# Attention and a gated MLP on one core: a list scheduler for all engines, half-blocks of 64 keys in eight array tiles, norms on VectorE and DMA

## The chip, the cores and the metric

One NeuronCore of a Trainium2 chip runs the whole kernel. Its engines work at the same time and are kept together by semaphores: TensorE (PE in the profile; its weight loads are PEld) multiplies from SBUF into PSUM, VectorE (DVE) and ScalarE (ACT) read PSUM, GpSimd (POOL) works on SBUF alone, and SyncE (SP) only issues DMAs. PSUM has eight banks of 128 partitions by 512 float32 values. TensorE's array can be used as a whole or as tiles of 32 or 64 rows or columns, each with weights of its own. The metric is the device time of one execution in microseconds (us), the median of several.

## The reference

With x of 2048 tokens by 512, the kernel computes x + A(xn) + B(xn), where xn is x normalised over its 512 features:

```
def _A_ref(x, wqkv, wo):
    H = 32; Dh = D // H; W = 256
    q, k, v = qkv[0], qkv[1], qkv[2]
    scores = jnp.einsum("bhqd,bhkd->bhqk", q, k) * (Dh ** -0.5)
    mask = (idx[:, None] - idx[None, :] >= 0) & (idx[:, None] - idx[None, :] < W)
    p = softmax(where(mask, scores, -1e9))
    return einsum("bhqk,bhkd->bhqd", p, v) ... @ wo
def _B_ref(x, w_gate, w_up, w_down):
    return ((x @ w_gate) * (x @ w_up)) @ w_down
```

There are 32 heads of 16 features, a causal window of 256 keys, and a hidden width of 1792. Inputs and output are bf16.

## The kernel before

Tokens go in four chunks of 512, and a chunk's work has two strands. The attention strand handles a chunk T, a group c of eight heads and a parity par of the heads (24 steps to a chunk). A score step (`scores`, L201) multiplies blocks of 128 keys with the queries that see them, for four heads at once: head e sits on 32 partitions, so four row tiles of the array (`tile_position=(32*e, 0)`) work side by side, each into a PSUM bank of its own. `Ko` is K with the even heads set to zero, which picks the odd head of a 32-row tile. The three steps of a parity (`GROUPS`) cover the twelve visible blocks in strips of 512 columns. ACT takes the exponential of the strip into P (L209), POOL sets the masked triangles to zero (L214, L218), and two steps later `values` (L234) multiplies P with V on four column tiles into the bank `accb`; a seventeenth column of ones gives the softmax's sum. DVE transposes the result in squares of 32 (L245), divides (L247, L248) and after both parities transposes back into `OT` (L251).

The dense strand is a list of "fillers" with costs in matmuls (`fillers`): projections (`proj_v`, `proj_qk`), 14 gate and up pairs (`gate`, `up`; DVE copies the gate to `gsb`, then multiplies the up sum by it into `hT`), the down sums with the output projection added in the same bank (`down`, `finish`), the result added to x and stored (`store`). The next chunk's norms hang between gates: `norm_stats`, `norm_scale`, `norm_apply`, and `norm_transpose`, which transposes xn on TensorE and copies it to `xnT`. Dense work shares three PSUM banks (`ps_m`), S has four, `accb` one.

The order is that of the program: `run` emits the first chunk's norms and projections block by block, then for each step the scores, the values of two steps before, and as many fillers as keep their share of the whole. Every engine executes its instructions in the order in which they were emitted. Loads of x and the MLP weights go through SP's queue, Wqkv in three parts through ACT's. Down sums of the last chunk run without the last head group; `finish_late` adds that part from a bank of its own.

## Time and profile before

| | |
|---|---|
| time, median of 3 runs | 301.23 us (301.23 to 304.61) |
| span of the profiled execution | 299.1 us, from the first to the last instruction |
| what lies around the span (median less span) | 2.1 us |
| busy: TensorE, DVE, ACT, POOL | 92%, 65%, 61%, 52% of the span |
| granted TensorE clock, mean | 0.996 |

The span is what the trace shows; the time of a run also has the start and end of the execution around it. Busy times of matmuls are their recorded durations, and since matmuls are pipelined, the price of one is read from start to start. The rest of the document uses "dense" for matmuls on the whole array.

### The profile page before, as it was taken

The page shows a single profiled execution, that of the slowest core. Times are in us where ns is not written, and L with a number is a line of the kernel's source. Part 1 is how long each engine was busy: PE and PEld are TensorE (multiplying, and loading weights), DVE is VectorE, ACT ScalarE, POOL GpSimd, SP SyncE. Part 2 cuts the span into 40 slices and gives each one's busy share as a digit, 9 for nine tenths or more (in the row PEclk, how much of TensorE's full clock was granted, in tenths as well). Part 3 has the DMA queues.
Part 4 walks back from the last instruction along what each step waited for, and adds up shares of the span by engine and source line. Part 5 has one row for each costly group of instructions (what it writes and reads, how often), then busy time and mean ns, then how long its engine had stood idle before and what let it go on. Part 6 is the DMA issues. An engine that isn't in the chain of part 4 may idle for free.

```text
span 299.1 us, 5877 instructions
## 1 busy us (share of the span) xinstructions
PE 274.7 (92%) x2424; PEld 119.6 (40%) x2460; DVE 194.3 (65%) x362; ACT 181.5 (61%) x118; POOL 156.8 (52%) x266
## 2 busy tenths in 40 slices
PE   6569989999999999999999999999999999999992
PEld 5333333433433444444344444443444443344440
DVE  3238898985823599984942489985763357877325
ACT  1247566568766756669566666758766675756610
POOL 3115565455565556656555466655556555555620
PEclk9999999999999999999999999999999999999998
DMA  7999000000000100000000000000000000000001
GB/s 234 370 369 324 3 3 0 3 0 2 1 20 18 37 0 2 1 2 2 0 19 19 20 18 3 0 2 1 2 0 20 35 20 1 2 0 2 2 0 70
DMA packets 10506, 12.17 MB, mean 41 GB/s; under 512 B 496, under 2 KB 10480, under 8 KB 10480
## 3 DMA queue, kind: packets, MB, share of 16 engines
q1 hardware_dynamic: 8896, 10.23, 10.1%
q10 hardware_dynamic: 1584, 1.57, 1.7%
q8 instruction: 19, 0.31, 0.4%
q14 instruction: 7, 0.06, 0.1%
HBM read 9.70 MB, written 2.10 MB: 39 GB/s over the span
## 4 chain that ended last, share of the span: by engine, by line
PE 68%; ACT 17%; DVE 6%; DMA 3%; issue 3%; POOL 1%; ACTq 1%; DVEq 0%
ACT P L209 16%; PE psd L279 15%; PE up L270 12%; PE gp L261 11%; PE S L201 10%; PE accb L234 7%; PE qkp L167 6%; DMA Wqkv<-in_A_wqkv_dram 3%; PE vp L157 2%; PE psd L284 2%; DVE at L245 1%; PE xTp L145 1%; DVE hT L272 1%; DVE st L114 1%; PE qkb L183 1%
## 5 line engine op out<-in xcount | busy, mean ns | idle before, releaser
L209 ACT ACTIVATE P<-S 128x2048 bf16<-128x2048 f32 (+2 forms) x96 | 170.0, 1771 | 86.8 <-PE S L201 79.1
L214 POOL TENSOR_SCALAR_AFFINE_SELECT P<-P 128x512 bf16<-128x512 bf16 x128 | 81.8, 639 | 75.2 <-ACT P L209 74.6
L218 POOL TENSOR_SCALAR_AFFINE_SELECT P<-P 128x512 bf16<-128x512 bf16 x112 | 72.8, 650 | 42.4 <-ACT P L209 42.4
L261 PE MATMUL gp<-xnT,Wg 128*128 128x512 bf16 x213 | 57.1, 380 | 1.4 <-DVE gsb L264 0.5
L270 PE MATMUL up<-xnT,Wu 128*128 128x512 bf16 x216 | 57.3, 380 | 0.5
L279 PE MATMUL psd<-Wd,hT 128*128 128x512 bf16 x213 | 51.7, 380 | 1.4 <-issue 1.3
L272 DVE TENSOR_TENSOR hT<-up,gsb 128x512 bf16<-128x512 f32 x56 | 38.5, 687 | 11.0 <-PE up L270 8.0
L245 DVE STREAM_TRANSPOSE at<-accb 128x512 f32<-128x512 f32 x32 | 22.9, 715 | 32.6 <-PE accb L234 32.2
L264 DVE CAST gsb<-gp 128x512 bf16<-128x512 f32 x56 | 38.1, 680 | 3.7 <-PE gp L261 3.4
L270 PEld LDWEIGHTS <-Wu 128*128 128x128 bf16 x224 | 19.9, 98 | 25.8 <-issue 5.4
L279 PEld LDWEIGHTS <-hT 128*128 128x128 bf16 x224 | 19.8, 97 | 25.9 <-issue 5.3
L261 PEld LDWEIGHTS <-Wg 128*128 128x128 bf16 x224 | 19.8, 98 | 25.0 <-issue 6.0
L167 PE MATMUL qkp<-xnT,Wqkv 128*128 128x512 bf16 x117 | 27.5, 380 | 0.5 <-issue 0.5
L234 PE MATMUL accb<-P,V 128*17 128x384 bf16 (+2 forms) x704 | 25.4, 276 | 0.0
L291 DVE TENSOR_TENSOR y<-psd,x 128x512 bf16<-128x512 f32 x12 | 8.3, 692 | 23.2 <-PE psd L284 23.2
L201 PE MATMUL S<-Q,Ko 32*128 32x256 bf16 (+2 forms) x352 | 18.4, 275 | 3.8 <-ACT P L209 3.6
L201 PE MATMUL S<-Q,K 16*128 16x256 bf16 (+2 forms) x352 | 18.4, 275 | 2.6 <-ACT P L209 2.4
L234 PEld LDWEIGHTS <-V 128*17 128x17 bf16 x704 | 13.8, 90 | 8.7 <-issue 5.5
L167 PEld LDWEIGHTS <-Wqkv 128*128 128x128 bf16 x120 | 10.7, 98 | 13.7 <-issue 2.5
L157 PE MATMUL vp<-Wqkv,xnT 128*128 128x512 bf16 x61 | 15.9, 392 | 0.3 <-issue 0.2
L201 PEld LDWEIGHTS <-Ko 32*128 32x128 bf16 x352 | 6.9, 92 | 22.6 <-issue 22.1
L201 PEld LDWEIGHTS <-K 16*128 16x128 bf16 x352 | 6.6, 92 | 22.6 <-issue 22.5
(44 smaller groups left out, 172.2 us busy)
## 6 DMA issues: line engine op xcount, KB each, us to landing
out_dram<-y SPq DMA_DIRECT2D x16, 128.0 KB, 1.7
Wg<-in_B_w_gate_dram SPq DMA_DIRECT2D x2, 896.0 KB, 9.9
Wu<-in_B_w_up_dram SPq DMA_DIRECT2D x2, 896.0 KB, 11.5
Wd<-in_B_w_down_dram SPq DMA_DIRECT2D x1, 1792.0 KB, 17.7
Wqkv<-in_A_wqkv_dram ACTq DMA_DIRECT2D x3, 512.0 KB, 6.0
x<-in_A_x_dram SPq DMA_DIRECT2D x1, 1024.0 KB, 14.6
x<-in_A_x_dram SPq DMA_DIRECT2D x4, 128.0 KB, 5.1
x<-in_A_x_dram SPq DMA_DIRECT2D x1, 512.0 KB, 8.2
```

Source lines behind the costliest of these rows:

```text
L167: nc.tensor.matmul(ps[:], lhsT=self.Wqkv[:, k, lo:lo + 128], rhs=self.xnT[T][:, k, :], start=(k == 0), stop=(k == 3))
L201: nc.tensor.matmul(S[:, e, col:col + n], lhsT=(self.Ko if par else self.K)[U][rows, c, 128 * j:128 * j + 128], rhs=self.Q[T][rows, c, 128 ...
L209: nc.scalar.activation(out=P[:, :, lo:hi], in_=S[:, :, lo:hi], func=ACT.Exp, scale=0.25)
L214: nc.gpsimd.affine_select(out=P[:, :, j:j + 128], in_=P[:, :, j:j + 128], pattern=[[0, 4], [1, 128]], compare_op=ALU.is_ge, fill=0.0, base ...
L218: nc.gpsimd.affine_select(out=P[:, :, j:j + 128], in_=P[:, :, j:j + 128], pattern=[[0, 4], [-1, 128]], compare_op=ALU.is_gt, fill=0.0, bas ...
L234: nc.tensor.matmul(acc[32 * e:32 * e + 17, 128 * q0:128 * q0 + n], lhsT=self.V[U][:, v, 8 * c + 2 * e + par, 0:17], rhs=P[:, e, col:col + ...
L245: nc.vector.transpose(out=at.rearrange("p b r -> p (b r)"), in_=acc[:])
L261: nc.tensor.matmul(ps[:], lhsT=self.Wg[:, k, 128 * f:128 * f + 128], rhs=self.xnT[T][:, k, :], start=(k == 0), stop=(k == 3))
L264: nc.vector.tensor_copy(out=self.gsb[:], in_=ps[:])
L270: nc.tensor.matmul(ps[:], lhsT=self.Wu[:, k, 128 * f:128 * f + 128], rhs=self.xnT[T][:, k, :], start=(k == 0), stop=(k == 3))
L272: nc.vector.tensor_tensor(out=self.hT[T][:, f, :], in0=ps[:], in1=self.gsb[:], op=ALU.mult)
L279: nc.tensor.matmul(self.psd[:], lhsT=self.hT[T][:, f, 128 * b:128 * b + 128], rhs=self.Wd[:, f, :], start=(f == 0), stop=False)
```

## The change

The whole program is written anew, around a scheduler in the file. `Op`, `Dense` and `Sums` are pieces of work with their inputs, engines and costs; `loop` places them one after another by estimated times (`choose` picks what TensorE does next: values, scores, or dense work from two lists A and B), and emits each when it is placed. So the order on every engine comes from the file's costs. Copies from PSUM may go to DVE or ACT, whichever the estimates favour. Four things change in the work itself.

Blocks of keys are 64 wide. `layout` deals the half-blocks to two lanes, even and odd, and a batch holds 512 columns of each lane: five batches for a pair (T, c) in chunks 1 to 3, four in chunk 0. Scores use eight tiles of 32 rows by 64 columns, values eight of 64 rows by 32 columns. In phase 0 of a pair's values lane 0 does the even heads and lane 1 the odd ones, each into its own bank, in phase 1 the other way round; TensorE is drained between the phases and a semaphore, `turn`, holds phase 1 back. A pair's two transposes, the reciprocal, the product and the transpose back follow together on DVE. POOL's selects work on one lane's 64 partitions and may span several half-blocks.

PSUM has S (four banks) and four banks M for everything else; a value pair takes two of them. The first chunk goes by blocks, with the third part of Wqkv moved to SP's queue. Later norms no longer pass through TensorE: DVE applies them, and `dma_start_transpose` on SP's queue writes `xnT`. In the last chunk the four down sums wait in four banks and Wo is added to them in place.

```diff
+    order = {
+        (0, 0): ((0, 2), (2, 4, 6)), (0, 1): ((1, 3), (3, 5, 7)),
+        (1, 0): ((-4, -2, 4), (0, 2), (2, 6)), (1, 1): ((-3, -1, 3), (1, 3), (5, 7)),
+    }
...
+    if T == 0:
+        plan = [((par, n, 0),) for par in range(2) for n in range(2)]
+    else:
+        plan = [((0, 0, 0),), ((0, 1, 0),), ((0, 2, 0), (1, 2, 4)), ((1, 0, 0),), ((1, 1, 0),)]
...
+        self.M = [psum.tile([128, 512], F32, name=f"M{i}") for i in range(4)]
...
-        for t in range(4):
-            nc.sync.dma_start(out=self.x[:, t, :], in_=xv[:, t, :])
-        for lo in (1024, 512, 0):
-            nc.scalar.dma_start(out=self.Wqkv[:, :, lo:lo + 512], in_=wq[:, :, lo:lo + 512])
-        nc.sync.dma_start(out=self.x[:, 4:8, :], in_=xv[:, 4:8, :])
+        load(nc.sync, self.x[:, 0, :], xv[:, 0, :])
+        load(nc.scalar, self.Wqkv[:, :, 1024:1536], w["qkv"][:, :, 1024:1536])
+        load(nc.sync, self.x[:, 1, :], xv[:, 1, :])
+        load(nc.scalar, self.Wqkv[:, :, 512:1024], w["qkv"][:, :, 512:1024])
+        load(nc.sync, self.x[:, 2, :], xv[:, 2, :])
+        load(nc.sync, self.x[:, 3, :], xv[:, 3, :])
+        load(nc.sync, self.Wqkv[:, :, 0:512], w["qkv"][:, :, 0:512])
...
-                nc.tensor.matmul(S[:, e, col:col + n],
-                                 lhsT=(self.Ko if par else self.K)[U][rows, c, 128 * j:128 * j + 128],
-                                 rhs=self.Q[T][rows, c, 128 * q0:128 * q0 + n],
-                                 start=True, stop=True, tile_position=(32 * e, 0),
-                                 skip_group_check=True)
+        for at, lane, par, k, q, m in sorted(todo):
+            U, j = divmod(8 * T + k, 8)
+            for e in range(4):
+                rows = slice(32 * e, 32 * e + (32 if par else 16))
+                self.nc.tensor.matmul(
+                    self.S[64 * lane:64 * lane + 64, e, 64 * at:64 * (at + m)],
+                    lhsT=(self.Ko if par else self.K)[U % 3][rows, c, 64 * j:64 * j + 64],
+                    rhs=self.Q[T % 2][rows, c, 64 * q:64 * (q + m)],
+                    start=True, stop=True, tile_position=(32 * e, 64 * lane), skip_group_check=True)
...
-                    nc.gpsimd.affine_select(out=P[:, :, j:j + 128], in_=P[:, :, j:j + 128],
-                                            pattern=[[0, 4], [1, 128]], compare_op=ALU.is_ge,
-                                            fill=0.0, base=0, channel_multiplier=-1)
+    def i_select(self, P, lane, kind, at, n, step):
+        v = P[64 * lane:64 * lane + 64].rearrange("p e (b q) -> p e b q", q=64)
+        v = v[:, :, at:at + (n - 1) * step + 1:step, :]
+        sign = -1 if kind else 1
+        self.nc.gpsimd.affine_select(out=v, in_=v, pattern=[[0, 4], [0, n], [sign, 64]], base=0, fill=0.0,
+                                     compare_op=ALU.is_gt if kind else ALU.is_ge, channel_multiplier=-sign)
...
-                    nc.tensor.matmul(acc[32 * e:32 * e + 17, 128 * q0:128 * q0 + n],
-                                     lhsT=self.V[U][:, v, 8 * c + 2 * e + par, 0:17],
-                                     rhs=P[:, e, col:col + n], start=first, stop=(i == 2),
-                                     tile_position=(0, 32 * e), skip_group_check=True)
+        if phase == 1:
+            self.nc.tensor.wait_ge(self.turn, self.v)
+        todo = []
+        for lane in range(2):
+            par, at0 = lane ^ phase, 0
+            for P, batch in strips:
+                for p, k, q, m, at in batch[lane]:
+                    if p == par:
+                        todo.append((at0, lane, par, k, q, m, at, P))
+                        at0 += m
+        for _, lane, par, k, q, m, at, P in sorted(todo, key=lambda t: t[:2]):
+            U, j = divmod(8 * T + k, 8)
+            for e in range(4):
+                self.nc.tensor.matmul(
+                    banks[par][32 * e:32 * e + 17, 64 * q:64 * (q + m)],
+                    lhsT=self.V[U % 3][64 * lane:64 * lane + 64, j // 2, 8 * c + 2 * e + par, 0:17],
+                    rhs=P[64 * lane:64 * lane + 64, e, 64 * at:64 * (at + m)],
+                    start=(par, e) not in begun, stop=phase == 1, tile_position=(64 * lane, 32 * e),
+                    skip_group_check=True)
+                begun.add((par, e))
+        if phase == 0:
+            self.nc.tensor.drain().then_inc(self.turn, 1)
...
-        for g, s in enumerate(steps):
-            fill(-1, g)
-            self.scores(*s)
-            values(g - LAG)
-            done_w += weight[g]
-            fill(total * done_w / sum(weight), g)
+    def loop(self):
+        while True:
...
+                    at = max(t, self.free[e])
+                    key = (at + (0.3 if e == "A" and len(o.on) > 1 else 0.0), o.rank, t)
+                    if best is None or key < best[0]:
+                        best = (key, o, e, at)
+            p = self.choose()
+            if p is not None and (best is None or p[0] <= best[3]):
+                self.do(*p)
...
+                break
+            _, o, e, at = best
+            took, lat = o.on[e]
+            o.start, o.eng, o.end = at, e, at + lat + LAT
+            self.free[e] = at + took
+            self.waiting.remove(o)
+            self.log.append((at, e, took, o.name))
+            if self.live:
...
+        hi = 64 * max(s[4] + s[3] for lane in batch for s in lane)
+        took = 0.000833 * 4 * hi
+        ex = self.op(f"exp{g}", {"A": (took + 0.06, took + 0.18)}, [o], lambda e: self.nc.scalar.activation(
+            out=P[:, :, 0:hi], in_=self.S[:, :, 0:hi], func=ACT.Exp, scale=0.25), rank=0)
...
+        for par in range(2):
+            t = self.op(f"tr{v}", {"V": (0.64, 0.74)}, [o] + ts, lambda e, par=par: nc.vector.transpose(
+                out=self.at[:, :, par, :], in_=self.M[banks[par]].rearrange("p (b r) -> p b r", r=32)), rank=1)
+            self.frees(t, banks[par])
+            ts = [t]
...
-        for k in range(4):
-            nc.tensor.transpose(ps[:, k, :], xn[:, 128 * k:128 * k + 128], self.ident[:])
...
+        st = [self.op(f"st{T}.{b}", {"V": (0.81, 0.9)}, begin, lambda e, b=b: self.i_stats(4 * T + b, self.mv[w]),
+                      rank=8) for b in range(4)]
...
+            ap = self.op(f"ap{T}.{b}", {"V": (0.32, 0.41)}, [r], lambda e, b=b: self.i_apply(4 * T + b), rank=7)
+            deps = [ap] + ([("up", T - 2, NF - 1)] if T > 1 else [])
+            self.at_["xnT", T, b] = self.op(f"dt{T}.{b}", {"S": (1.5, 3.0)}, deps, lambda e, b=b: (
+                self.nc.sync.dma_start_transpose(out=self.xnT[w][:, :, 128 * b:128 * b + 128], in_=self.xn[b][:])),
+                rank=1)
...
-        for b in range(4):
-            self.finish_late(NCH - 1, b)
+        late = [] if b < 2 else [("attended", T)]
+        self.B.insert(len(self.B) - b, Sums(name, T, b, 0, NF, h + late, 7, emit, lambda o, i: None, link))
+        self.B.append(Sums("wo" + name, T, b, NF, 18, o, 4, emit, evac, link))
```

DVE at the start, from the first statistics on (`st`; `mv` holds mean and variance, `xn` the normalised block, `qkb` the first K and Q sums). Before:

```order
L114 BN_STATS st_169<-x_87 128x6
L115 BN_AGGR mv_168<-st_169 128x2
L114 BN_STATS st_177<-x_87 128x6
L115 BN_AGGR mv_176<-st_177 128x2
L133 TENSOR_SCALAR xn_184<-x_87,mv_168,rs_174 128x512
L185 CAST K0_164<-qkb_193 128x128
L186 CAST Q0_163<-qkb_193 128x128
L114 BN_STATS st_211<-x_87 128x6
L115 BN_AGGR mv_210<-st_211 128x2
L133 TENSOR_SCALAR xn_218<-x_87,mv_176,rs_182 128x512
```

The third block's statistics stand behind the first block's K and Q. DVE at the same place after the change:

```order
L267 BN_STATS st_189<-x_64 128x6
L268 BN_AGGR mv0_98<-st_189 128x2
L267 BN_STATS st_192<-x_64 128x6
L268 BN_AGGR mv0_98<-st_192 128x2
L267 BN_STATS st_197<-x_64 128x6
L268 BN_AGGR mv0_98<-st_197 128x2
L278 TENSOR_SCALAR xn0_94<-x_64,mv0_98,rs0_100 128x512
L267 BN_STATS st_203<-x_64 128x6
L268 BN_AGGR mv0_98<-st_203 128x2
L278 TENSOR_SCALAR xn1_95<-x_64,mv0_98,rs0_100 128x512
L278 TENSOR_SCALAR xn2_96<-x_64,mv0_98,rs0_100 128x512
L278 TENSOR_SCALAR xn3_97<-x_64,mv0_98,rs0_100 128x512
```

All four statistics and applies now come ahead of the first copy of K; the third block's statistics stand ahead of the first apply. SP's queue from the last loads on, before:

```order
L69 DMA x_87<-in_A_x_dram 128x8x512
L70 DMA Wd_92<-in_B_w_down_dram 128x14x512
L71 DMA Wo_89<-in_A_wo_dram 128x4x512
L292 DMA out_0_dram<-y_1140 128x512
L292 DMA out_0_dram<-y_1220 128x512
```

The stores follow the loads directly. SP at the same place after the change:

```order
L168 DMA Wo_66<-in_A_wo_dram 128x4x512
L632 DMA_TRANSPOSE xnT1_82<-xn0_94 128x4x128
L632 DMA_TRANSPOSE xnT1_82<-xn1_95 128x4x128
L632 DMA_TRANSPOSE xnT1_82<-xn2_96 128x4x128
L632 DMA_TRANSPOSE xnT1_82<-xn3_97 128x4x128
L632 DMA_TRANSPOSE xnT0_81<-xn0_94 128x4x128
L632 DMA_TRANSPOSE xnT0_81<-xn1_95 128x4x128
L632 DMA_TRANSPOSE xnT0_81<-xn2_96 128x4x128
L713 DMA out_0_dram<-y_1632 128x512
L632 DMA_TRANSPOSE xnT0_81<-xn3_97 128x4x128
L713 DMA out_0_dram<-y_1843 128x512
```

Two chunks' transposes stand ahead of the first stores, and one store stands within the second four.

## Rows read from the trace of the kernel before

**Rows 1.** The page: busy us, and the chain that ended last, by engine.
```profile
PE 274.7 (92%) x2424; PEld 119.6 (40%) x2460; DVE 194.3 (65%) x362; ACT 181.5 (61%) x118; POOL 156.8 (52%) x266
...
PE 68%; ACT 17%; DVE 6%; DMA 3%; issue 3%; POOL 1%; ACTq 1%; DVEq 0%
```

**Rows 2.** Windows: stretch, its us, busy us of each engine, clock, DMA.
```profile
21.40:294.30 272.90, 261.72 (x2326) 111.01 (x2360) 185.14 (x335) 175.99 (x109) 152.26 (x249) 1.00 0.05 17
0.00:21.40 21.40, 12.90 (x98) 8.61 (x101) 7.58 (x25) 5.56 (x9) 4.51 (x17) 1.00 0.97 323
```

**Rows 3.** The chain in order of time: start, us, what.
```profile
283.95 3.02 PE psd L279 x14
```

**Rows 4.** Timeline of PE, 100 to 105.9 us: start, us, instructions, idle before.
```profile
100.15 0.40 PE L201 MATMUL S<-Q,K 16*128 16x384 bf16 x8
...
102.61 0.40 PE L201 MATMUL S<-Q,Ko 32*128 32x128 bf16 x8 [0.23 <-ACT P L209]
102.94 1.04 PE L270 MATMUL up<-xnT,Wu 128*128 128x512 bf16 x4
...
104.68 1.03 PE L270 MATMUL up<-xnT,Wu 128*128 128x512 bf16 x4
105.64 0.40 PE L201 MATMUL S<-Q,Ko 32*128 32x256 bf16 x8
```

**Rows 5.** Timeline of PE, 105.5 to 108.5 us.
```profile
105.96 0.83 PE L234 MATMUL accb<-P,V 128*17 128x128 bf16 x24
106.73 1.04 PE L261 MATMUL gp<-xnT,Wg 128*128 128x512 bf16 x3
```

**Rows 6.** Waits of PE: us in total, times, longest us.
```profile
PE S L201 <- ACT P L209: 6.1, 23, 0.6
```

**Rows 7.** The four matmuls that begin the value step: durations (ns), and the timeline.
```profile
L234 PE MATMUL accb<-P,V x4: 224/224/226, 106.0 to 106.0; 128*17 128x128 bf16 x4
...
105.96 0.23 PE L234 MATMUL accb<-P,V 128*17 128x128 bf16 x4
```

**Rows 8.** DMA issues: count, KB each, median us to landing.
```profile
out_dram<-y SPq DMA_DIRECT2D x16, 128.0 KB, 1.7
...
x<-in_A_x_dram SPq DMA_DIRECT2D x4, 128.0 KB, 5.1
```

**Rows 9.** Timeline of DVE, 5 to 21.6 us, and PE's first score step.
```profile
5.58 0.69 DVE L114 BATCH_NORM_STATS2 st<-x 128x6 f32<-128x512 bf16 x1 [1.36 <-DMA x<-in_A_x_dram]
...
11.01 0.29 DVE L185 CAST K<-qkb 128x128 bf16<-128x128 f32 x1 [4.23 <-PE qkb L183]
...
11.42 0.68 DVE L114 BATCH_NORM_STATS2 st<-x 128x6 f32<-128x512 bf16 x1
...
12.23 0.38 DVE L133 TENSOR_SCALAR xn<-x,mv,rs 128x512 bf16<-128x512 bf16 x1
14.61 0.29 DVE L185 CAST K<-qkb 128x128 bf16<-128x128 f32 x1 [1.99 <-PE qkb L183]
...
21.40 0.34 PE L201 MATMUL S<-Q,K 16*128 16x384 bf16 x4
```

**Rows 10.** Groups by line and shape: busy us, mean ns of one, idle before.
```profile
L209 ACT ACTIVATE P<-S 128x2048 bf16<-128x2048 f32 x80 | 150.2, 1878 | 76.8 <-PE S L201 69.1 <-POOL P L218 6.4 <-POOL P L214 1.3
L214 POOL TENSOR_SCALAR_AFFINE_SELECT P<-P 128x512 bf16<-128x512 bf16 x128 | 81.8, 639 | 75.2 <-ACT P L209 74.6
...
L264 DVE CAST gsb<-gp 128x512 bf16<-128x512 f32 x56 | 38.1, 680 | 3.7 <-PE gp L261 3.4
...
L245 DVE STREAM_TRANSPOSE at<-accb 128x512 f32<-128x512 f32 x32 | 22.9, 715 | 32.6 <-PE accb L234 32.2
...
L78 POOL TENSOR_SCALAR_AFFINE_SELECT ident<-ident 128x128 bf16<-128x128 bf16 x1 | 0.3, 292 | 0.1
```

**Rows 11.** Timeline of DVE at the end: the last four results.
```profile
293.31 1.87 DVE L291 TENSOR_TENSOR y<-last,y 128x512 bf16<-128x512 f32 x3
295.83 0.69 DVE L291 TENSOR_TENSOR y<-last,y 128x512 bf16<-128x512 f32 x1 [0.66 <-DMA out_dram<-y]
```

More of the change, by code (lines that the diff above doesn't have):

```diff
@@ new lines, in selects @@
+def selects(batch):
+    out = []
+    for lane in range(2):
+        cols = {0: [], 4: []}
+        for _, k, q, m, at in batch[lane]:
+            for i in range(m):
+                if q + i - k in cols:
+                    cols[q + i - k].append(at + i)
+        for d, cs in cols.items():
+            cs.sort()
+            while cs:
+                run, step = 1, (cs[1] - cs[0] if len(cs) > 1 else 1)
+                while run < len(cs) and cs[run] - cs[run - 1] == step:
+                    run += 1
+                if run * step != 8:
+                    run = step = 1
+                out.append((lane, d // 4, cs[0], run, step))
+                cs = cs[run:]
+    return out
@@ new lines, in copy, with matmuls, i_scores @@
+    def copy(self, eng, out, in_):
+        if eng == "A":
+            self.nc.scalar.activation(out=out, in_=in_, func=ACT.Copy)
+        else:
+            self.nc.vector.tensor_copy(out=out, in_=in_)
+    def matmuls(self, ps, pairs, first=True, last=True):
+        for n, (a, b) in enumerate(pairs):
+            self.nc.tensor.matmul(ps, lhsT=a, rhs=b, start=first and n == 0, stop=last and n == len(pairs) - 1)
+    def i_scores(self, T, c, batch):
+        todo = [(at, lane, par, k, q, m) for lane in range(2) for par, k, q, m, at in batch[lane]]
+        for at, lane, par, k, q, m in sorted(todo):
+            U, j = divmod(8 * T + k, 8)
@@ new lines, in pe, with take_bank, frees, f @@
+    def pe(self, at, took, name, reader="V"):
+        o = Op(name, {}, [], None)
+        o.start, o.end = at, at + took + PE_LAT[reader]
+        self.now = at + took
+        self.log.append((at, "P", took, name))
+        return o
+    def take_bank(self):
+        i = min((t, i) for i, t in enumerate(self.banks) if t is not None)[1]
+        self.banks[i] = None
+        return i
+    def frees(self, op, i):
+        def f(o):
+            self.banks[i] = o.end
+        op.then.append(f)
+    def score_deps(self, g):
+        T, c, batch = self.batches[g]
+        deps = {("S", g - 1), ("Pfree", g - self.PBUFS)}
+        for lane in range(2):
+            for par, k, q, m, at in batch[lane]:
+                U, j = divmod(8 * T + k, 8)
+                deps |= {("Ko" if par else "K", U, c, j // 2), ("Q", T, c, q // 2), ("Q", T, c, (q + m - 1) // 2)}
+        return [d for d in deps if not (d[0] in ("S", "Pfree") and d[1] < 0)]
```

760 lines of the change are left out of this document (450 added, 310 removed), and 3 rows, old and new, of the table GROUPS.

## Prediction

> **What bounds the kernel now.** I read the page's busy shares and its chain first. TensorE is busy 92% of the span and holds 68% of the chain that ended last; no other engine passes 65% [rows 1]. Then the stretches: from the first score matmul (21.40 us) to the last matmul TensorE's records cover 261.7 of 272.9 us, at a granted clock of 1.00, 2.4 GHz [rows 2]. So in the body each microsecond is a slot of TensorE's, and the question is how many slots the change removes. The other places are the start, where TensorE is busy 12.9 of 21.4 us [rows 2], and the end, 4.9 us without matmuls.
>
> The timeline gives the price of a slot. Fourteen dense matmuls of 512 columns take 3.02 us, 0.216 each [rows 3]; 128 columns are then 0.054. A score step of 512 columns on each of four row tiles holds TensorE from 102.61 to 102.94, 0.33: its columns and 0.11 more. Four dense matmuls (0.86) ahead of a score step take 104.68 to 105.64, so going over costs 0.10 [rows 4]. A value step (1536 columns on each of four column tiles) takes 105.96 to 106.73, 0.77: 0.65 and 0.12 [rows 5]. I take 0.11 for each change between dense, score and value work.
>
> The ledger of the body before: 904 dense matmuls after the first score step (920 less the 16 of the first chunk's V), 195.0 us; 48 transposes of 128 columns, 2.6; scores, 80 steps of 512 columns, 8 of 384 and 8 of 256, 46,080 columns, 19.4; values, 24 steps of 1536 and 8 of 1152, again 46,080, 19.4; 225 changes, counted in the instruction order, 24.8. The sum is 261.2; the stretch is 272.9, so 11.7 us are waits. The largest is scores that wait for the exponential still reading S: 6.1 us in 23 waits [rows 6].
>
> **The change part by part.**
>
> *Half-blocks.* With blocks of 64 keys the band has less waste: a pair (a chunk and a group of eight heads) needs 20 half-blocks of 64 columns for each lane and parity where it had 12 blocks of 128. Two lanes side by side make 76 score batches of 512 columns for 96 steps: 38,912 columns, 16.4 us, 3.0 less. The values need 2560 columns a pair in chunks 1 to 3 and 2048 in chunk 0: 38,912 again, 3.0 less. This holds if eight tiles run at once. The trace has four at once, by rows and by columns, never both; I take full overlap, since each split by itself shows no cost beyond its columns and the change of mode [rows 4, 5]. The other end, no overlap, is a rival.
>
> *Small matmuls.* There are 3328 tiled matmuls for 1408. The four that begin a value step last 0.224 each and together 0.23 [rows 7]: their starts lie some 3 ns apart, so the 22 of a batch need about 0.07 of its 0.216 us, and the number costs nothing. The Trainium skill ("TensorE: Matmul & The Clock Gate", section "Wait — 56ns, not 53.3ns?") says that start-to-start never drops below about 25 ns, however small a matmul is. By that rule 3328 of them need 83 us, an estimate from the page, and the sum would end 50 us higher; the trace disagrees for matmuls on different tiles, with its 3 ns.
>
> *Changes of mode.* The new order has 198 for 225: 3.0 less. Sixteen drains of TensorE are new, one between the phases of each value pair. No drain is in the trace. Below, it costs nothing beyond the change that follows anyway; above I put 0.5, an estimate of two emptyings by the 0.22 to 0.23 that one small matmul lasts [rows 7]. It is nearest to a change of mode, so I take 0.15 each, 2.4.
>
> *Later norms by DMA.* 48 transposes leave TensorE, 2.6 us; nine of their copies leave DVE. Twelve DMA transposes of 128 KB are new, on SP. The nearest rows are the output stores of that size, 1.7 us to landing, and the x loads, 5.1 [rows 8]. Behind the last of chunk 1's applies the new order has nineteen gate and up groups ahead of the first projection that reads xnT1, 16.4 us, with seven score batches and two value pairs besides, some 21 us. Four transposes one after another take 6.8 by the stores and 20.4 by the loads, so they are hidden; above I allow 3 us, once (the later chunks have about 40 us). Stores queue behind them on SP and y has three buffers, but the transposes are issued before the next chunk's sums are due.
>
> *The start.* Before, DVE has the third block's statistics (11.42) behind block 0's copy of K, which waits 4.23 us; the blocks then go one after another, and the first scores start at 21.40 [rows 9]. The new order has all statistics early. But the third stands ahead of the first apply, and its x lands late: the second's statistics start at 5.58 [rows 9], and the median landing is 5.1 after an issue at some 2 to 3 us [rows 8], so I put the third at 7.9. Statistics to apply take 0.81, apply to the copy of K 2.38 [rows 9], and block 0's V now stands between, 0.86: 12.0. From there DVE has eleven copies up to block 2's Q, six of 128 columns at 0.29 [rows 9] and five of 512 at up to 0.68 [rows 10], 5.1 us: 17.1. I take 17.5 for the first scores; the ends are 16.1 (the third block lands a little sooner) and 21.4 (nothing gained).
>
> *The waits.* By slots, scores in the new order start at least 2.55 us apart; two that ACT alone holds apart start 2.46 apart (100.15 and 102.61, [rows 4]). So the 6.1 us should go; the other 5.6 stay. New is that a value pair holds two of four accumulators, where dense work had three to itself; I add 3, so 8.6.
>
> *Other engines.* ACT: 76 exponentials for 96, 142.7 us at 1.88 [rows 10], and 14 copies, less than before. DVE: ten gate casts and nine xnT copies go, fifteen V copies come, reciprocals and products are merged, some 9 us off its 194. POOL: 357 selects on 64 partitions for 240, 301 of them of 256 elements and 56 of 512; a select of 128 elements took 0.29, one of 512 0.64 [rows 10], so 0.41 and 0.64: 159 us, as now, off the path except as a rival.
>
> *The end.* Now the fourth y waits for a buffer and starts 3.3 us before the span ends [rows 11]. In the new order 49 dense matmuls, 10.6 us, and the sixteen of Wo follow the last values, so OT is ready in time and the y's follow sums 0.86 apart: 3.5 us behind the last matmul if no y waits for a buffer, 4.9 as now; I take 4.0.
>
> **The sum.** Dense 195.0, block 3's K and Q after the first scores 0.4, scores and values 32.8, 198 changes 21.8: 250.0. With 17.5 ahead, 2.4 of drains, 8.6 of waits and 4.0 behind it, the span is 282.5, for 299.1. The profiled execution's span lies 2.1 us under the median of 301.23, so the prediction is **284.6 us**, 5.5% less. Its own range: start -1.4 to +3.9, drains -2.4 to +5.6, waits -5 to +8, transposes up to +3; not all on one side, so 276 to 293.
>
> **The rivals.**
>
> *The lanes run one after the other* (slower). Scores use two column halves of one row group at once, values two row halves of one column group. If such a pair shares a path, the columns double: 32.8 us more, 317. It decides from an overlap under a half: then more than the 16.6 us gained are lost. For: the trace has no such pair. Against: four columns' streams cross all rows at once today, and four row groups' all columns [rows 4, 5]. Chance 0.07.
>
> *A floor per matmul* (slower). The 24 matmuls of a value step in 0.65 us are 27 ns each, which could be a price per matmul and not of columns: 3328 would then take 90 us for 32.8, 342. Against it stand the starts 3 ns apart [rows 7]: 0.02. The Trainium skill's page named above states such a floor; with its 25 ns the time would be 335.
>
> *DVE sets the pace.* The order is fixed, so an engine that is late makes all behind it late. Both transposes of a pair (0.715 each, [rows 10]) stand together ahead of dense copies while two accumulators are left: up to 1.4 us a pair. At 1.0 for 16 pairs 16 us, of which 3 are counted: 298. For: DVE stays 66% busy, with stretches nearly full. Against: before, transposes stood ahead of the same copies, and dense matmuls hardly waited. Chance 0.11, half of it under 295.
>
> *POOL falls behind.* If a select costs 0.64 whatever its size, a pair of chunks 1 to 3 has some 26, 16.8 us, about what TensorE needs for one; the values wait for masks, up to 10 us: 289 to 295. Against: 0.29 for the select of 128 elements [rows 10]. Chance 0.04.
>
> *Hardly any wait.* With 2 us of waits, no price of drains and a start at 16.1 the time is 274. Chance 0.03.
>
> **How the numbers follow.** The forecast has the other 0.73. Faster than 295.2 (by over 2%, about what a measurement of this kernel can tell from no change) are the forecast, the last case, half of DVE's and most of POOL's: 0.85. Within 2%: the rest of those two, 0.06. Slower: the first two, 0.09. The range 275 to 297 leaves out the slower cases, the last one and a tail of DVE's, under 0.2.
>
> **What would show it.** Right: first scores near 17.5 us; a score batch from its start to the next dense matmul about 0.33, a value phase about 0.65; TensorE over 95% busy in the body; S hardly waiting for ACT. Wrong: a batch of 0.55 or a phase of 1.2 (lanes in turn); dense matmuls that wait for DVE over 10 us in sum; values waiting for POOL; chunk 1's first projection waiting for a DMA.

## The result and the profile after

The changed kernel takes **281.54 us** (median of 4 runs, 281.14 to 282.16), the kernel before 301.23 beside it: a ratio of 0.931, 95% interval 0.926 to 0.937, so 6.9% less. The prediction was 284.6, its range 275 to 297. Beside the experiments below, the fast runs of the kernel before took 300.47 to 305.05 us, so a difference of one or two us from it is within its scatter. The changed kernel was not run again beside them.

The page of the kernel after, busy time by engine, the instruction queue of the DMAs, and the chain that ended last:

```profile
span 279.4 us, 9843 instructions
...
PE 266.8 (96%) x4336; PEld 122.7 (44%) x4336; DVE 183.9 (66%) x323; ACT 150.8 (54%) x91; POOL 210.9 (75%) x447
...
q8 instruction: 34, 0.56, 0.9%
...
PE 83%; POOL 9%; DMA 2%; DVE 2%; issue 2%; ACT 1%; SPq 0%; ACTq 0%
```

ACT held 17% of the chain before [rows 1]; now it holds 1%, TensorE 83%. POOL went the other way: it is busy three quarters of the span where it was busy half, and holds 9% of the chain for 1%. The next rows are the windows of the three stretches: up to the first score step, up to the end of the last matmul's slot, and behind it:

```profile
0.00:18.15 18.15, 12.23 (x97) 8.75 (x97) 10.22 (x29) 2.68 (x4) 4.23 (x17) 0.91 0.93 315
18.15:275.40 257.25, 254.47 (x4241) 113.93 (x4240) 173.01 (x293) 148.08 (x87) 206.69 (x430) 1.00 0.12 31
275.40:279.40 4.00, 0.13 (x1) 0.00 (x0) 0.69 (x2) 0.00 (x0) 0.00 (x0) 0.97 0.29 98
```

The span lost 19.7 us: 3.25 in the start (21.40 before, [rows 2]), about 15.6 in the body, 0.9 at the end. What TensorE waits for in the body, by the view of waits from 18.2 us on, is one line:

```profile
PE M L255 <- POOL P L236: 0.5, 2, 0.3
```

Before it had 6.1 us behind ACT alone [rows 6]. Three pieces of TensorE's timeline: a score step between dense groups, the two phases of a value pair, and the score step again in a window that ends 0.03 us behind its start:

```profile
110.13 1.03 PE L218 MATMUL M<-xnT,Wu 128*128 128x512 bf16 x4
111.09 0.42 PE L226 MATMUL S<-Q,Ko 32*64 32x320 bf16 x16
111.44 1.04 PE L218 MATMUL M<-xnT,Wg 128*128 128x512 bf16 x4
...
117.19 0.74 PE L255 MATMUL M<-P,V 64*17 64x64 bf16 x56
118.08 0.42 PE L226 MATMUL S<-Q,K 16*64 16x320 bf16 x16
118.43 0.77 PE L255 MATMUL M<-P,V 64*17 64x128 bf16 x56
119.13 1.04 PE L218 MATMUL M<-xnT,Wg 128*128 128x512 bf16 x4
...
111.09 0.34 PE L226 MATMUL S<-Q,Ko 32*64 32x320 bf16 x8
```

Eight matmuls of 320 columns, some 0.318 us each, fit in 0.34: the eight tiles work at once. The step holds TensorE from 111.09 to 111.44, about 0.36. The phases differ: 117.19 to 118.08 is 0.89, with the drain at its end, and 118.43 to 119.13 is 0.70, without. A step's price is read from its start to the start of what comes next; its listed duration runs some 0.07 us further (111.09 and 0.42, but the next start is 111.44). Summed over the body from the starts of the steps: 76 score steps 27.1 us, 32 value phases 25.3, and the dense groups between them 190.8, that is 0.216 for each matmul and 0.10 for each time TensorE comes back to them. The groups of instructions that moved most:

```profile
L236 POOL TENSOR_SCALAR_AFFINE_SELECT P<-P 64x256 bf16<-64x256 bf16 x368 | 167.0, 475 | 33.7 <-ACT P L498 25.4
L498 ACT ACTIVATE P<-S 128x2048 bf16<-128x2048 f32 x76 | 142.6, 1877 | 86.8 <-PE S L226 77.7 <-POOL P L236 9.1
...
L236 POOL TENSOR_SCALAR_AFFINE_SELECT P<-P 64x512 bf16<-64x512 bf16 x56 | 37.2, 673 | 7.1 <-ACT P L498 6.1
```

The exponentials are as long as before (1.88, [rows 10]) and 76 for 96. The selects are 424 on 64 partitions, and one of 256 elements costs 0.475.

So three candidates share the gain: the start, the transposes that left TensorE, and the body, where half-blocks and the scheduler's order came together. **The theory** to be tested: the start and the transposes are gains by themselves, and the half-blocks pay because 76 exponentials leave room between the scores where 96 did not; on TensorE itself they bring little. **Rivals**: the scheduler's order took the waits away, whatever the blocks; or the half-blocks' fewer columns are what pays.

### The profile page after: what moved, and what is told of

Same layout as the page of the kernel before. It is cut to its first block, busy times and chain, and to the rows that moved or that the text cites. A ratio compares the mean times of both kernels' runs of the same rounds, so it can differ in the third digit from the quotient of the medians.

```text
span 279.4 us, 9843 instructions
## 1 busy us (share of the span) xinstructions
PE 266.8 (96%) x4336; PEld 122.7 (44%) x4336; DVE 183.9 (66%) x323; ACT 150.8 (54%) x91; POOL 210.9 (75%) x447
## 3 DMA queue, kind: packets, MB, share of 16 engines
q1 hardware_dynamic: 15952, 12.32, 15.6%
## 4 chain that ended last, share of the span: by engine, by line
PE 83%; POOL 9%; DMA 2%; DVE 2%; issue 2%; ACT 1%; SPq 0%; ACTq 0%
PE M L218 68%; PE S L226 9%; POOL P L236 8%; PE M L255 6%; DMA x<-in_A_x_dram 2%; ACT P L498 1%; POOL rs L273 0%; PE M L592 0%; SPq L168 0%; DVE xnT L214 0%; DVE st L267 0%; DVE hT L688 0%; DVE gsb L214 0%; DVE V L214 0%; DVE y L709 0%
## 5 line engine op out<-in xcount | busy, mean ns | idle before, releaser
L236 POOL TENSOR_SCALAR_AFFINE_SELECT P<-P 64x256 bf16<-64x256 bf16 (+1 forms) x424 | 202.9, 501 | 40.7 <-ACT P L498 31.5
L498 ACT ACTIVATE P<-S 128x2048 bf16<-128x2048 f32 x76 | 142.6, 1877 | 86.8 <-PE S L226 77.7
L218 PE MATMUL M<-xnT,Wu 128*128 128x512 bf16 x224 | 57.7, 380 | 0.1
L218 PE MATMUL M<-xnT,Wg 128*128 128x512 bf16 x224 | 57.7, 380 | 0.0
L218 PE MATMUL M<-Wd,hT 128*128 128x512 bf16 x224 | 54.5, 380 | 0.5
L688 DVE TENSOR_TENSOR hT<-M,gsb 128x512 bf16<-128x512 f32 x56 | 37.9, 677 | 10.6 <-PE M L218 10.2
L532 DVE STREAM_TRANSPOSE at<-M 128x512 f32<-128x512 f32 x32 | 21.2, 696 | 25.7 <-PE M L255 25.5
L214 DVE CAST gsb<-M 128x512 bf16<-128x512 f32 x46 | 31.5, 686 | 7.2 <-PE M L218 6.7
L218 PE MATMUL M<-xnT,Wqkv 128*128 128x512 bf16 (+1 forms) x152 | 31.0, 351 | 0.0
L218 PEld LDWEIGHTS <-hT 128*128 128x128 bf16 x224 | 19.8, 98 | 24.9 <-issue 2.8
L255 PE MATMUL M<-P,V 64*17 64x192 bf16 (+4 forms) x1664 | 23.6, 240 | 0.5 <-POOL P L236 0.5
L218 PEld LDWEIGHTS <-Wqkv 128*128 128x128 bf16 x152 | 13.4, 101 | 14.3 <-issue 0.9
L226 PEld LDWEIGHTS <-Ko 32*64 32x64 bf16 x832 | 8.1, 104 | 13.4 <-issue 13.4
```

Source lines behind the costliest of these rows:

```text
L214: self.nc.vector.tensor_copy(out=out, in_=in_)
L218: self.nc.tensor.matmul(ps, lhsT=a, rhs=b, start=first and n == 0, stop=last and n == len(pairs) - 1)
L226: self.nc.tensor.matmul(self.S[64 * lane:64 * lane + 64, e, 64 * at:64 * (at + m)], lhsT=(self.Ko if par else self.K)[U % 3][rows, c, 64 * ...
L236: self.nc.gpsimd.affine_select(out=v, in_=v, pattern=[[0, 4], [0, n], [sign, 64]], base=0, fill=0.0, compare_op=ALU.is_gt if kind else ALU ...
L255: self.nc.tensor.matmul(banks[par][32 * e:32 * e + 17, 64 * q:64 * (q + m)], lhsT=self.V[U % 3][64 * lane:64 * lane + 64, j // 2, 8 * c + ...
L498: ex = self.op(f"exp{g}", {"A": (took + 0.06, took + 0.18)}, [o], lambda e: self.nc.scalar.activation(out=P[:, :, 0:hi], in_=self.S[:, :, ...
```

## The experiments

**128-key blocks under the scheduler.** The half-blocks alone are undone; start, scheduler and DMA transposes stay. A head parity's three steps take the place of a lane pair's, HOLD is 0.5, and the scheduler's other numbers (WINDOW 6, PACE 2.45, SHARE 0.6) are those with which its own plan for such blocks ends first. The drain is gone with the second phase.

```diff
-            batches = layout(T)
+            batches = layout(T)[3 * par:3 * par + 3]
...
-                    self.S[64 * lane:64 * lane + 64, e, 64 * at:64 * (at + m)],
+                    self.S[:, e, 128 * at:128 * (at + m)],
...
-            self.nc.tensor.drain().then_inc(self.turn, 1)
...
-            if s is not None and s <= now:
-                return now, "S", None
+            if s is not None and s <= now + self.HOLD:
+                return max(s, now), "S", None
```

> The changed kernel's scheduler, start and DMA transposes with the blocks of before: 128 keys, four tiles, 96 score steps and as many exponentials, no drain. The scheduler was told to hold TensorE for a score step that is due within 0.5 us. My theory, that TensorE itself gains about nothing from the half-blocks (6.0 us of columns and 2.8 of changes against 3.0 of drains and 5.3 of dearer small matmuls) and that they pay by leaving 20 exponentials out: scores that ACT holds 2.46 us apart leave 2.0 us for dense work in quanta of 0.86, so some 0.3 us are lost at most of the 96 steps; about 295 to 303 us, waits of 15 to 25 us back on scores behind ACT. Rival, the scheduler's order is what removed the waits whatever the blocks: 281 to 286 us, waits of some 1 to 3 us.

294.95 us (294.44 to 295.22; 0.977 of before). Its view of waits in the body:

```profile
PE S L185 <- ACT P L442: 8.9, 39, 0.3
PE M L178 <- issue: 2.5, 16, 0.2
```

Without the half-blocks 13.4 of the 19.7 us are gone again (14.1 by the two traces' bodies, from the first score step to the last matmul; the start is 0.8 shorter here), and 39 waits for the exponential are back, in an order made by the same scheduler. Half of the distances between score steps are 2.50 us or less; in the changed kernel the shortest is 2.62 and the mean 3.14. The time is at the low end of what was expected for the theory and the listed waits, 8.9 us, are below the 15 to 25 expected; the order by itself does not do it. (A record of a matmul is missing here and there in this trace; the "issue" line is such gaps.)

**The same, with shorter exponentials.** This one asks whether the 13.4 us are ACT's or TensorE's. It leaves out a quarter of most exponentials, so it is a probe and no usable kernel. The edit is shown against the run above.

```diff
-            out=P[:, :, lo:hi], in_=self.S[:, :, lo:hi], func=ACT.Exp, scale=0.25), rank=0)
+            out=P[:, 0:4 if g < 31 else 3, lo:hi], in_=self.S[:, 0:4 if g < 31 else 3, lo:hi], func=ACT.Exp, scale=0.25), rank=0)
...
-            last = self.op(f"sel{g}", {"G": (cost, cost + 0.06)}, [ex, last], lambda e, m=m: self.i_select(P, *m), rank=1)
+            last = self.op(f"sel{g}", {"G": (cost, cost + 0.06)}, [ex, last], lambda e, m=m: self.i_select(P, *m, 4 if g < 17 else 3), rank=1)
```

> The kernel of 128-key blocks under the scheduler (294.95) in the same order, with exponentials shorter by a quarter: from step 31 on, 65 of 96, the fourth head of each is left out and keeps an older step's values, and its masks are left out from step 17 on. Theory, with 96 steps the exponentials pace the scores (half of the distances between them are 2.46 to 2.50 us) and hold TensorE some 12.9 us in sum: two thirds of that go, 6 to 9 us less, 286 to 289. Rival, the blocks of 128 are dear on TensorE itself: 0 to 2 us less.

286.42 us (286.22 to 287.21), 8.5 less, inside 6 to 9. The line of waits, and then the group of the shortened exponentials (65 of the 73; eight had this length before):

```profile
PE S L185 <- ACT P L442: 2.6, 12, 0.2
```

```profile
L442 ACT ACTIVATE P<-S 128x1536 bf16<-128x1536 f32 x73 | 105.9, 1451 | 75.3 <-PE S L185 62.6 <-POOL P L194 12.7
```

TensorE's instructions are the same in number, shape and order, so the 8.5 us are waits for the exponential. The list fell by 6.3 only; it counts a wait from the listed end of the last matmul, so it leaves out some 0.07 us at each, 1.9 at the 27 that went. 2.6 are left, in the 31 steps that kept their length, or 3.4 with what the list leaves out. Taking them off too leaves 283.0, 1.5 above the changed kernel, which has some 1.1 us of waits itself: an estimate of what blocks of 128 cost TensorE itself, beyond the half-blocks, is 2 to 3 us of the 13.4. The masks that went with the fourth head shorten POOL as well; the view lists no wait of TensorE's body for POOL in either run.

**Longer exponentials in the changed kernel.** The opposite dose: a second, shorter exponential ahead of each, in the order of the changed kernel.

```diff
-        ex = self.op(f"exp{g}", {"A": (took + 0.06, took + 0.18)}, [o], lambda e: self.nc.scalar.activation(
-            out=P[:, :, 0:hi], in_=self.S[:, :, 0:hi], func=ACT.Exp, scale=0.25), rank=0)
+        ex = self.op(f"exp{g}", {"A": (took + 0.06, took + 0.18)}, [o], lambda e: [self.nc.scalar.activation(
+            out=P[:, :, 0:n], in_=self.S[:, :, 0:n], func=ACT.Exp, scale=0.25) for n in (128, hi)], rank=0)
```

> The changed kernel, in the same order, with a second exponential of 128 columns a head (512 elements) ahead of each of the 76: about 0.55 us more in which S isn't free, worked out from an ACT operation of 512 elements at 0.60. Theory, the half-blocks pay because 76 steps leave slack between scores: in the changed kernel's trace 30 of 75 distances between score steps are under 3.0 us and lack 9.6 us in sum, so 3 to 10 us more, where each step would pay 0.55, 42 us, if ACT set the pace throughout. Rival, ACT has no part in the time any more: 0 to 1 us.

> The same with 256 columns a head more (1024 elements), about 1.0 us a step. Theory, the slack is used up: 58 of 75 distances are under 3.45 us and lack 34 us in sum; 25 to 35 us more, waits of scores for ACT back. Rival, ACT has no part: 0 to 2 us.

299.04 us (297.98 to 299.19) and 323.34 (322.94 to 323.82): 17.5 and 41.8 us more. The first lies above what was expected, the second too. The waits of the two, and the chain of the second:

```profile
PE S L226 <- ACT P L498: 14.0, 37, 0.5
```

```profile
PE S L226 <- ACT P L498: 39.3, 58, 1.0
```

```profile
ACT 52%; PE 35%; issue 5%; POOL 3%; DMA 2%; DVE 1%; ACTq 0%; SPq 0%; POOLq 0%
```

The miss was the shortest distance between scores, which I had put at 3.0 and 3.45 us. In these traces, where ACT alone holds two steps apart, they start 3.17 and 3.60 apart. With these two values the same sum over the changed kernel's 75 distances (what each lacks to the shortest possible one) gives 18.0 and 43.1 us, against 17.5 and 41.8 measured. So the rule of the theory holds at both doses, with shortest distances that were read from these two traces and not known ahead: a step costs nothing as long as its neighbours are further apart than the exponential allows, and costs all that is lacking from there. The rule also says how near the changed kernel lies to that edge: 0.6 us more in an exponential would cost most of the gain.

**The start alone.** The kernel before with only its first chunk's statistics, applies and transposes earlier.

```diff
-        self.norm_stats(0, 1)
-        self.norm_scale(0, 1)
         for b in range(4):
+            self.norm_stats(b, 1)
+            self.norm_scale(b, 1)
+            if b:
+                self.norm_apply(b - 1)
+        self.norm_apply(3)
+        self.norm_transpose(0, True)
+        for b in range(4):
             if b < 3:
-                self.norm_stats(b + 1, 1)
-                self.norm_scale(b + 1, 1)
-            self.norm_apply(b)
-            self.norm_transpose(b, True)
+                self.norm_transpose(b + 1, False)
```

> The kernel before with only its first chunk's work in another order: statistics and applies early, transposes one block ahead. Theory, the start is a gain by itself that everything behind inherits: first scores at some 18.5 us for 21.40 and 2.5 to 3 us less, 298.3. Rival, the body behind it has its own bound by the exponentials and takes the start back as waits: first scores early, time within 0.5 us of before.

296.40 us (296.19 to 296.66; 0.982 of before, 0.976 to 0.988): 4.8 less. The first scores start at 17.3 us for 21.40 [rows 9], so 4.1 of it is the start itself. The rival, that the body takes it back, falls: TensorE waits for ACT 5.8 us in 23 waits here, 6.1 in 23 before [rows 6]. My size was low: statistics early and transposes one block ahead gain 4.1 us together, which this run does not divide. The two profiled spans differ by 4.4 (299.1 and 294.8); the rest of the 4.8, which is counted from 301.23, is within the scatter of the kernel before.

**Later norms on TensorE again.** Each block's four transposes and one copy go into the dense work of the chunk before.

```diff
-            self.at_["xnT", T, b] = self.op(f"dt{T}.{b}", {"S": (1.5, 3.0)}, deps, lambda e, b=b: (
-                self.nc.sync.dma_start_transpose(out=self.xnT[w][:, :, 128 * b:128 * b + 128], in_=self.xn[b][:])),
...
+            self.turns[T].append((f"turn{T}.{b}", 1.1, deps, turn, turned))
```

> The changed kernel with the later norms' 48 transposes on TensorE again, and their twelve copies on DVE or ACT, set among the dense work by the same scheduler. Theory, what TensorE is given costs its time: 48 x 0.054 = 2.6 us more, with waits for the copies up to 4; 284.1 to 285.5. Rival, they fall into idle time or the DMA transposes cost a hidden wait: within 0.5 us of the changed kernel.

284.35 us (283.87 to 285.12): 2.8 more, as 48 x 0.054 = 2.6 says. The DMA transposes are hidden: in the changed kernel's list of DMA issues they take 3.6 us, and no matmul waits for one.

```profile
xnT<-xn SPq DMA_TRANSPOSE x12, 3.6
```

**A second drain.**

```diff
         if phase == 0:
             self.nc.tensor.drain().then_inc(self.turn, 1)
+        else:
+            self.nc.tensor.drain()
```

> The changed kernel with a second drain of TensorE behind each value pair's second phase, where the next matmuls change the mode anyway: sixteen more. Theory, a drain holds TensorE for what the last matmuls need to end, beyond a change of mode, some 0.19 us as the first phases show it: 16 x 0.19 = 3.0 us more, 284.5. Rival, the drain hides under the change of mode, and what the first phases show is the wait for the turn: 0 to 0.5 us more.

285.45 us (284.72 to 285.93): 3.9 more, 0.24 for each drain on average, a little above the 0.19 of the first phases. Two value phases of chunk 0 in the timeline; the second held TensorE from 47.55 to 48.11 in the changed kernel, 0.56, and here:

```profile
47.46 0.41 PE L226 MATMUL S<-Q,K 16*64 16x128 bf16 x24
47.80 0.62 PE L255 MATMUL M<-P,V 64*17 64x320 bf16 x40
48.64 0.39 PE L218 MATMUL M<-xnT,Wg 128*128 128x512 bf16 x1 [0.21 <-issue]
```

from 47.80 to 48.64, 0.84. A drain is not covered by the change of mode behind it. A version without drains wasn't tried.

**Lanes in turn.** Score and value matmuls are issued lane by lane.

```diff
-        for at, lane, par, k, q, m in sorted(todo):
+        for at, lane, par, k, q, m in sorted(todo, key=lambda t: (t[1], t[0])):
-        for _, lane, par, k, q, m, at, P in sorted(todo, key=lambda t: t[:2]):
+        for _, lane, par, k, q, m, at, P in sorted(todo, key=lambda t: (t[1], t[0])):
```

> The changed kernel with the score and value matmuls of a step issued lane by lane, all of lane 0 and then all of lane 1, in place of both lanes in turn. Theory, eight tiles work at once and only because neighbours in the order are on different tiles: a score batch takes about 0.57 for 0.36, a value phase 1.2 to 1.4 for 0.70, together some 25 to 35 us more, with part of it hidden where TensorE has slack: 305 to 315. Rival, TensorE looks far enough ahead, or the lanes were never at work together: no more than 1 us.

287.02 us (one run): 5.5 more, between the two expectations. A score step, in a window that ends 0.04 us behind its start and then in a whole one:

```profile
102.36 0.35 PE L226 MATMUL S<-Q,K 16*64 16x320 bf16 x8
...
102.36 0.44 PE L226 MATMUL S<-Q,K 16*64 16x320 bf16 x16
102.73 0.61 PE L218 MATMUL M<-Wd,hT 128*128 128x512 bf16 x2
```

In the program four matmuls of 192 columns for lane 0 stand between lane 0's four of 320 and lane 1's. All eight of 320 have started within 0.04 us all the same: here TensorE does not hold the next tile's matmul back behind one whose tile is busy. Undisturbed score steps of 16, 24 and 32 matmuls take 0.37, 0.39 and 0.40 us, where they took 0.356, 0.359 and 0.364. In the value phases a lane has 20 to 28 matmuls, and there they lose about 0.15 each (32 phases take 32.3 us, against 27.5 in the runs whose traces lack as many records).

**All tiled matmuls of 64 columns.**

```diff
+        todo = [(at + i, lane, par, k, q + i, 1) for at, lane, par, k, q, m in todo for i in range(m)]
         for at, lane, par, k, q, m in sorted(todo):
...
+        todo = [(a0 + i, lane, par, k, q + i, 1, at + i, P) for a0, lane, par, k, q, m, at, P in todo for i in range(m)]
         for _, lane, par, k, q, m, at, P in sorted(todo, key=lambda t: t[:2]):
```

> The changed kernel with every score and value matmul cut into matmuls of 64 columns, on the same tiles in the same order: 9728 for 3328, the same columns. It measures what a small matmul costs. If each has a price in TensorE's issue: the extra 6400 at 7 ns each (what the changed kernel's 5.3 us over 3328 and the columns of a batch leave open goes from 2 to 7) are 13 to 45 us more. Rival, only columns count: within 1 us. Rival, a floor of some 25 ns for each: 160 us more.

406.03 us (one run): 124.5 more. It does not measure one thing. The trace has 9600 tiled matmuls, 4800 for scores and 4800 for values, and not the 9728 that I had counted. In the timeline an undisturbed first value phase of 160 such matmuls and an undisturbed score step of 64 hold TensorE 1.61 and 0.63 us, 10 ns each, where they took 0.89 and 0.36:

```profile
181.32 1.47 PE L257 MATMUL M<-P,V 64*17 64x64 bf16 x160
182.93 0.70 PE L227 MATMUL S<-Q,K 16*64 16x64 bf16 x64
183.56 0.19 PE L257 MATMUL M<-P,V 64*17 64x64 bf16 x1
```

Were all 76 steps and 32 phases undisturbed, they would take some 42 us more, 6.7 ns for each of the 6272 added matmuls. That is an estimate from such steps; it lies inside the 13 to 45 that a price in TensorE's issue was to cost. The other 80 us are something else.

The view of waits has a line for the value matmuls:

```profile
PE M L257 <- issue: 47.1, 25, 2.7
```

And windows of 1 us show TensorE's matmuls grow few, its granted clock fall, and every engine idle in one of them:

```profile
113.00:114.00 1.00, 0.21 (x26) 0.09 (x26) 0.00 (x0) 0.00 (x0) 0.95 (x3) 1.00 0.48 57
114.00:115.00 1.00, 0.60 (x69) 0.61 (x70) 0.00 (x0) 0.00 (x0) 1.00 (x3) 0.63 0.01 1
115.00:116.00 1.00, 0.76 (x83) 0.62 (x69) 0.00 (x0) 0.00 (x0) 0.02 (x1) 0.50 0.06 16
116.00:117.00 1.00, 0.00 (x0) 0.00 (x0) 0.00 (x0) 0.00 (x0) 0.00 (x0) 0.50 0.00 0
```

In the stretches behind the stops the granted clock lies at 0.50, 1.2 GHz, and dense matmuls take longer there: a group of twelve up to 4.97 us for 2.69. (How the 124.5 us divide can't be read from the starts of the steps: 91 of the 912 dense records are missing, and where the first of a group is, the step ahead looks 0.23 us longer.) The 47.1 us of stops lie in the value phases, with 160 matmuls in a row, and the page's instruction queue (q8) moves 1.36 MB for 0.56; that TensorE had run out of instructions is the reading that fits, but no run here isolates it. What follows for the changed kernel: its score steps have 16, 24 or 32 matmuls and take 0.356, 0.359 and 0.364 us, so at these numbers a matmul more costs half a nanosecond. The price of some 7 ns appears only with more of them; that it does where the columns no longer cover it is a reading, not shown by a run between. The Trainium skill ("TensorE: Matmul & The Clock Gate", section "Wait — 56ns, not 53.3ns?") has start-to-start never below about 25 ns; 64 matmuls in 0.63 us on eight tiles lie under that.

**Two numbers of the scheduler.**

```diff
-    WINDOW = 4
+    WINDOW = 5
-    SHARE = 1.0
+    SHARE = 0.8
```

> The changed kernel with two of the scheduler's numbers changed: it looks five groups of dense work ahead in place of four, and gives the down projection 0.8 of its share, so more of it is left for the end. Theory, only 1.1 us of waits and 3.3 us of start are left to win for an order: between 1.5 us faster and 0.5 slower, 280.0 to 282.0. Rival, the order is still what sets the time: 3 us or more either way.

280.06 us (279.63 to 281.26), 1.5 less: the good end of what the theory leaves to an order. The slowest run here and the fastest of the changed kernel (281.14) meet, and the profiled spans differ by 0.7.

**Landing times as measured.**

```diff
-        land = (3.2, 3.6, 4.3, 4.7)
-        wv, wk, wq = 5.2, 6.6, 8.0
+        land = (3.2, 5.6, 7.5, 8.6)
+        wv, wk, wq = 5.2, 7.3, 9.6
```

> The changed kernel with the scheduler's landing times of the first four x blocks and of the three parts of Wqkv put where the trace shows them, so that block 0's apply stands ahead of the third block's statistics. Theory, the first scores come when the last x block and the DVE work behind it allow, and DVE's wait of 0.98 us for the third block moves but does not go: 0 to 1 us less. Rival, the wait was in the chain of the start: 1 us or more less, first scores near 17.

277.57 us (277.12 to 277.90; 0.916 of before): 4.0 less than the changed kernel, so the rival holds. DVE's timeline, first of the changed kernel, then of this one:

```profile
6.32 0.18 DVE L268 BATCH_NORM_AGGREGATE mv<-st 128x2 f32<-128x6 f32 x1
7.48 0.69 DVE L267 BATCH_NORM_STATS2 st<-x 128x6 f32<-128x512 bf16 x1 [0.98 <-DMA x<-in_A_x_dram]
8.21 0.18 DVE L268 BATCH_NORM_AGGREGATE mv<-st 128x2 f32<-128x6 f32 x1
8.31 0.38 DVE L278 TENSOR_SCALAR xn<-x,mv,rs 128x512 bf16<-128x512 bf16 x1
```

```profile
3.64 0.18 DVE L268 BATCH_NORM_AGGREGATE mv<-st 128x2 f32<-128x6 f32 x1
4.84 0.41 DVE L278 TENSOR_SCALAR xn<-x,mv,rs 128x512 bf16<-128x512 bf16 x1 [1.02 <-POOL rs L273]
5.38 0.69 DVE L267 BATCH_NORM_STATS2 st<-x 128x6 f32<-128x512 bf16 x1
```

The scheduler had believed in early blocks and put three statistics ahead of the first apply; DVE keeps to the order and waits. With the apply at 4.84 for 8.31 TensorE has block 0's work while the rest lands, and the first scores start at 15.19 for 18.15. That is the whole of it in the traces: the spans differ by 3.2 us (276.2 and 279.4), and the body is 0.2 shorter. The 4.0 between the medians has another 0.8 that no trace places.

**Both together.** The two edits above in one kernel.

> Both changes to the scheduler's numbers together: landing times as measured, window 5, share 0.8. Theory, the first gains in the start (first scores at 15.19 for 18.15 us) and the second in the body's waits, so they add: 4.0 and 1.5, 276. Rival, the landing times alone already took the body's waits: 277.2 to 277.9.

277.12 us (276.84 to 277.68, 6 runs; 0.915 of before, 0.910 to 0.920). By the medians they don't add: 0.4 less than the landing times alone, with overlapping runs. By the profiled spans they do: 3.2 and 0.7 less alone, 4.0 together. At this size the runs don't tell. The kernel beats both: 4.4 us, 1.6%, under the changed one.

## Why the prediction was right

**The whole.** Start -4.8 (made alone in the kernel before), transposes -2.8, half-blocks -13.4 are 21.0 for the 19.7 measured. With start and transposes in place, blocks of 128 under the scheduler end at 294.95, where 301.23 - 4.8 - 2.8 is 293.6. The 1.3 between is within the scatter of the kernel before, so these runs show no gain of the order by itself; it is the carrier of the rest. The two traces give a second division: start 3.3, waits of the body 10.3 (11.4 to 1.1), TensorE's own work 3.1, transposes 2.6 and end 0.9, less 0.4 for block 3's K and Q.

**Start.** Put at 17.5, measured 18.15. The mechanism was named rightly: the third block's statistics stand ahead of the first apply and wait for x. They were put at 7.9 and start at 7.48; block 0's copy of K was put at 12.0 and starts at 12.61, and behind it DVE waits for TensorE another 0.67 and 0.15 us, which a sum of durations leaves out.

**Half-blocks, columns.** The full overlap of eight tiles is right, and with it the rivals on lanes and on a floor per matmul are out. That the columns are 6 us fewer is right as a count. What failed is that each of the 198 changes costs 0.11. Read the same way in both traces (a step from its start to the next start, less its columns at the dense price of 0.216 for 512), a score step costs 0.141 us beyond its columns for 0.114 before, a value phase of chunks 1 to 3 0.160, without its drain, for 0.119, and a return to dense work 0.10 in both. Summed, the 198 changes are 24.9 us, as much as the 225 before: the 3.0 us of fewer changes went into dearer ones. It is not the number of matmuls in a step (16 to 32 made 0.008 us of difference); what else the steps pay for stays open. With 3.0 us for the drains (put at 2.4), TensorE's own work is 3.1 us less than before, where the prediction had 6.6 (6.0 and 3.0 less 2.4). The two runs with blocks of 128 say the same by another way, 2 to 3 us; ahead of the first of them I had put it at about nothing, since I set the dearer steps of the new kernel against a price of 0.103 that the steps before did not have either.

**Waits.** Put at 8.6, and the mis-sized term of the sum: 1.1 us, counting what the phases and steps of the body took beyond their usual length; the view has 0.5 of it, behind POOL's masks. The 6.1 us behind ACT went for the reason given, scores further apart. The other 5.6, which I let stay, went too. The view of before lists 1.9 us of them, behind DVE, and what it leaves out at the 23 waits for ACT is some 1.6 more; where the rest stood no run shows. The 3 us for the two accumulators never came: dense groups do not wait for DVE in the body. The waits were 7.5 us too many, the changes 3.1 and the drains 0.6 too few, and the start came 0.65 late: together that is the 3.1 by which the span came out shorter (279.4 for 282.5). That the errors have opposite signs is luck; the sum was better than its terms.

**Other engines.** ACT and DVE are as put (150.8 and 183.9 busy). POOL was wrong: 357 selects at 0.41 and 0.64, 159 us, where there are 424 at 0.475 and 0.673, 204. Nothing hung on it, since the values wait for POOL only 0.5 us; but POOL now stands at 75%, with 9.1 us of exponentials behind its selects.

**End.** 4.0 as put: the four y start 0.86 apart, the last at 275.57, and none waits for a buffer.

**The rivals on engines.** "DVE sets the pace" has no wait to show for it; "POOL falls behind" has the 0.5 us above, where the rival had up to 10. What stays open: whether another order for blocks of 128 keys would do better than 294.95. One scheduler and one set of its numbers were tried.

## What to carry to other kernels

Where one engine's step must wait for another's to free a single buffer, write down the distances between the steps, and the shortest distance that the second engine allows: the loss is the sum of what is lacking, and a restructuring that needs fewer steps can pay there though it saves the busiest engine little. Test it by lengthening and shortening the suspected step with the order held. And a schedule fixed in advance is as good as the arrival times that it believes in: here the true landing times were worth 4.0 us, two tuned numbers of its choice 1.5, and both together 4.4.

## What was unexpected of the hardware

- Matmuls on eight tiles start some 3 ns apart, and a matmul whose tile is busy does not hold back later ones for other tiles: with the lanes issued in turn a score step took 0.37 to 0.40 us for 0.36.
- A drain of TensorE costs 0.19 us behind a first value phase and 0.24 where it was doubled, on top of the 0.10 of the change of mode.
- With 9600 tiled matmuls of 64 columns TensorE takes 10 ns for each in undisturbed rows of 64 and 160; in other rows of 160 it stops for up to 2.7 us, and the granted clock falls to 0.50, 1.2 GHz. Why it stops is not isolated.
- A listed wait of TensorE is some 0.07 us short, since a matmul's listed end lies behind the start of the next (111.09 and 0.42 against 111.44): 8.5 us came back where the list fell by 6.3.
- A select on 64 partitions of 256 elements takes 0.475 us, where one on 128 partitions of 512 takes 0.64 [rows 10]: halving partitions and elements together saves a quarter. With 512 elements on 64 partitions it takes 0.673.
